# Down-sampled and banded attention followed by a gated expert layer on one core: nine equal token chunks instead of ten, with every queue written in a new order

## The chip, the cores and the metric

The kernel runs on 1 core of one Trainium2 chip. The metric is the device time of one execution in microseconds (us). TensorE is called PE, VectorE DVE, ScalarE ACT, GpSimd POOL, and SyncE, which issues all transfers here, SP. PE's clock has two levels, 1.2 and 2.4 GHz; the profile gives the level granted in a stretch as a share of the higher one.

## The reference

Attention runs over 8 batches of 8 heads, 576 positions and 64 values a head, and its result x (8 x 576 = 4608 tokens of 512 values) goes through a layer that mixes each token with the one before it:

```python
out_up    = repeat(softmax(mean4(q) @ mean4(k).T / 8) @ mean4(v), 4)   # per head
out_local = softmax(where(|i - j| < 4, q @ k.T / 8, -1e9)) @ v
x  = out_up + out_local                               # heads side by side: 512 values a token
xk = mu_k * x + (1 - mu_k) * x_prev                   # x_prev: the token before, in its batch
xr = mu_r * x + (1 - mu_r) * x_prev
k  = max(xk @ w_k, 0)                                 # 512 -> 1024
v  = (k * k) @ w_v                                    # 1024 -> 512
out = sigmoid(xr @ w_r) * v
```

## The kernel before, in words

**Attention.** The work is cut into 32 units n, two heads of one batch each; four units make a batch. For a unit, SP loads q, k and v (`load_raw`, `load_v4`, `load_windows`); the first six units turn q and k on PE (`flip`, L558) and copy the result out of the accumulation memory on ACT or DVE (`turn_part`, L423 and L427), later ones turn them on DVE. `run_pe(n)` issues in one piece on PE the scores of unit n (`score_pe`, L649 or L654), the down-sampled scores (L712) and the products of the unit before with its values (L805). DVE, ACT and POOL make the softmax, and `av_up`, `av_two` and `av_out` (L423, L877, L884) write the unit's part of x into one of two tiles `xt`, one a batch. After a batch's last unit, `av_pe` issues the value products alone.

**The layer.** The 4608 tokens are cut into chunks of 512 tokens (`CHUNKS`), two of them of 256 tokens only, at 2048 and at 4352. A chunk has one or two pieces of 256 tokens. For each piece DVE and ACT make xk and xr (`mix_prev`, `mix_part`), split into a high and a low part (`mix_high` L427 or ACT, `mix_low` L971), since every product is formed as high x high, high x low and low x high. For each of eight blocks f of w_k, `k_pe` (L983) issues twelve products whose moving operand is the whole chunk: 512 columns, or 256 in the two short chunks. ACT takes the maximum with 0, squares and rounds (L997, L1001, L1005), and DVE or POOL forms the low part (`k_low`, L1011). `v_pe` (L1040) issues, for a block f and a piece, six products of 512 columns, three for each of the piece's two tiles t of 128 tokens; they add up over f in one bank a tile. `r_pe` (L1020) issues twelve products of 512 columns a tile, `gate` (L1025) the sigmoid, `store_mul` (L1050) the last product on DVE, and `store_out` (L1054) the store. For the last tile of the program `columns` cuts the last block's products, the multiplication and the store in two halves of 256 columns.

**The weights.** Each of 20 weight tiles is loaded (L445), put together from two words on ACT and DVE (L450, L463, L467) and split into a high and a low part; for four of them PE forms the difference (`weight_diff`, L478 and L479). Before the program's first products, `warm` (L364) issues nine products of 512 columns on a cleared tile (`clear_warm`, L358).

**The order.** Every step is a task of a planner (`Plan.add`). The order in which tasks are issued, on all five engines, is a written-out list of task numbers (`ORDER`); `ELSE` moves named tasks to another engine. `Plan.arrange` walks that list, gives out the six accumulation banks, and the program then ties each engine's instructions into that order, so that every engine works strictly through its own queue. What waits for what follows from the data.

Of the kernel before, what the change touches and what calls it, by code (L numbers as in the profile page):

```python
# [51 lines left out]
0,4A5G1s5N0-3:1t5U5B5O0.5H490*1d5I151K4F4B1e5J4>1X5P3,5C165E4C1Y17184K1f4D4G5F5Q5Y0/4E1L505X1Z4r0:1a5Z4L5u5K5R5a
1M4t5L1N1b5v414s19591g1A4H1B4u5S1i3-3)4I5c1h4M1Q4J4N5n5V4v5d5o3<5e5f4O5h5p4P635g5i5z5y1O5j5q5k5W4w3&4Q3>1j1k4U64
5r1l5b1R1S6K4y1T5#4V4R654S5l3*5!1U5w4x3;5m1V5s4T5t5%6L661C3+1P4W1D4X6H3.424Y5+4z5&1m5(5,5x5)684!676N4Z1n5;6I3=69
5*5<6M815=4e5-5>5.6P607>615$4a6O6A4b4#4f6B4c826Q6C4d5/4$5:4g8U623/6R4h6D406E4%6S6T4i6U6V4j836k6J6X6q8V6d6o856m84
4l6Y6e8R6l6f6F6Z6n6G4&436r6p4(444k6s4)6u6t7=4m6w4p864+6&6g6W6+6)6(6-6*6a6h8S4*4n6i6,6!6.4q6b6j6/876c4o6:6x8E766#
8F6y8w6v8K7B774,8L8u788W888G6z8H8X8A8Y7Q8D8M807C8N8x798O7D8Z7L6$898P8B8Q4.4-967E8T8I8C8a7A8t8m7F7G8J8b8g8n8c8h8d
8e8y7s8z7H8o977M7t6%7N7I7u6;7J724/8i6=8#7K938j7v8f7k8p7O8!7R7SA&8k7P8v7x7l8q8l7w8r8s8$7T7U8;947y8%8<8+8&7zA#8(8,
70987V958*8-8)8.9ABC997a8=A(7W719B8>7X7#4;7b908/7Y8:917!7Z926<7c6>9C7d9OA$7$739D9P9E9FA)A%7%9QBF9G9I9V7mA*7e9X9J
BG9W9b9Z9c7f749K9a4:9YBh757nA+7&9d9f9HA,7g7o7h9g9h9e7i7j9p7(9R9r9t9l9v7)9L9w9u9S7q9m7p9s7+9q9M9x7*9i9N9j9T7r9UA-  # L60
9yA>BD9,BHB09k7-A:9n7,A=B59;9-BeBJB6B17.B7B2BiA6B89<A.BI9=9.B97;9/9oBKB,9>A1BA9:BBA/BfA;A<BLA2B37:BX7/B4AX9zBMBN
# [26 lines left out]
1!2J2p2x2>333V3Z3h565.6a8H8j8.9LBUBwC6E#FBF(HmH;IqKXKzL9Nk  # L88
""",
    DVE="""  # L90
0G0i0o0!0:1D1P1h1#1*1;2I2c2m2o2r32353D3M3Y3(3*3>494J4T4d555Z5!5&5:5<606s6y6/6;70727P8O8b8q8s8v8#8<959A9S9U9b9f9l
9z9#9%9(9*A+A,B6BEBJBYBbBlBoB(B+B;CACFCICMCOCQCSCWCiCkCsC:DsD!D&E7EpE(E+E:F0F1FFFKFNFkFmFvFxF,F/F;G3G5G7GFGHGJGL
GNGPGRGVHVHbHdHqHyH)I0IEIOISIXIfIgIuI$I)I+I/J2J4JAJIJfKGKLKMKOKeKjKoKrK%K+LGLLLRLiLpLrL#L(L<M5MQN7N9NINMNPNoNrNt
N+N=O4O6O8OAOGOKOMOOOQOSOUOWOYOaOvPWPaPcPePiPkPm
""",
    POOL="""
7A7F7K7U7eA5AKC+DAD<EMERGpGzG&JQJaJpMVOgOlOqO-O<PxP/P>Q9
# [9 lines left out]
class Plan:  # L107
# [64 lines left out]
    def lead(self, t, x):  # L172
# [148 lines left out]
def attention_moe(ctx: ExitStack, tc, q, k, v, mu_k, mu_r, w_k, w_v, w_r, band, ident, out):  # L321
# [706 lines left out]
    def v_pe(c, h, f):  # L1028
# [4 lines left out]
        if not (ended and c == NCH - 1):  # L1033
            todo.sort(key=lambda x: x[2] == 2)
# [140 lines left out]
    def both(keys):  # L1175
        return [x + y for y in keys for x in "hl"]
# [214 lines left out]
```

## Time and profile before

| | |
|---|---|
| time, median of 3 runs | 646.27 us (644.24 to 647.96) |
| profiled execution, its own time | 640.03 us |
| its span, first to last instruction | 638.2 us |
| instructions | 18038 |
| mean granted PE clock | 0.993 |
| bytes over HBM | 56.85 MB read, 13.86 MB written |

The span is what the page and the views of the trace describe; the profiled execution's own time is 1.8 us longer. Busy time of PE counts products whose ends are modelled; a matmul that is followed at once by another shows a longer time than the distance between their starts, so paces below are taken from starts.

### The profile page before, as it was taken

The page shows a single profiled execution, that of the slowest core. Times are in us where ns is not written, and L with a number is a line of the kernel's source. Part 1 is how long each engine was busy: PE and PEld are TensorE (multiplying, and loading weights), DVE is VectorE, ACT ScalarE, POOL GpSimd, SP SyncE. Part 2 cuts the span into 40 slices and gives each one's busy share as a digit, 9 for nine tenths or more (in the row PEclk, how much of TensorE's full clock was granted, in tenths as well). Part 3 has the DMA queues.
Part 4 walks back from the last instruction along what each step waited for, and adds up shares of the span by engine and source line. Part 5 has one row for each costly group of instructions (what it writes and reads, how often), then busy time and mean ns, then how long its engine had stood idle before and what let it go on. Part 6 is the DMA issues. An engine that isn't in the chain of part 4 may idle for free.

```text
span 638.2 us, 18038 instructions
## 1 busy us (share of the span) xinstructions
PE 621.7 (97%) x7034; PEld 514.7 (81%) x7034; DVE 483.5 (76%) x1039; ACT 400.1 (63%) x957; POOL 206.6 (32%) x285
## 2 busy tenths in 40 slices
PE   6799999999999999999999999999999999999997
PEld 5667788888888888888888888888888888888885
DVE  3969989888899979866799888978889757613133
ACT  3668867787677675766647576559667664334332
POOL 5757767536220451100430323012413320010110
PEclk9989999999999999999999999999999999999999
DMA  8888977556664656274354556635554330000001
GB/s 278 210 213 222 214 177 154 106 110 128 136 142 85 151 105 124 48 160 85 61 137 98 122 108 134 139 69 111 108 116 111 76 80 19 36 14 1 16 34 66
DMA packets 247127, 71.91 MB, mean 113 GB/s; under 512 B 219642, under 2 KB 238466, under 8 KB 247042
## 3 DMA queue, kind: packets, MB, share of 16 engines
q1 hardware_dynamic: 247042, 70.76, 49.4%
q8 instruction: 55, 0.90, 0.6%
q14 instruction: 30, 0.25, 0.1%
HBM read 56.85 MB, written 13.86 MB: 111 GB/s over the span
## 4 chain that ended last, share of the span: by engine, by line
PE 95%; issue 2%; DVE 1%; DMA 1%; ACT 0%; POOL 0%; SPq 0%; DVEq 0%; POOLq 0%
PE acc L1040 31%; PE ps_g L983 31%; PE ps_r L1020 16%; PE ps_v L805 5%; PE ps_a L712 3%; PE ps_a L649 3%; PE ps_f L558 1%; PE ps_a L654 1%; DMA wk<-in_moe_w_k_dram 1%; PE ps_m L926 1%; PE ps_w L478 1%; PE ps_t L762 1%; PE ps_t L767 0%; DVE ps_w L463 0%; ACT ad L729 0%
## 5 line engine op out<-in xcount | busy, mean ns | idle before, releaser
L983 PE MATMUL ps_g<-xks,wk 128*128 128x512 f32 (+1 forms) x960 | 206.9, 369 | 0.4 <-issue 0.4
L983 PEld LDWEIGHTS ps_g<-xks,wk 128*128 128x128 f32 x960 | 168.2, 188 | 32.6 <-issue 1.3
L1040 PE MATMUL acc<-wv,kh 128*128 128x512 f32 x578 | 157.3, 393 | 0.1
L1040 PEld LDWEIGHTS acc<-wv,kh 128*128 128x128 f32 x578 | 106.0, 188 | 21.9 <-PE ps_g L983 0.5
L1020 PE MATMUL ps_r<-wr,xr 128*128 128x512 f32 x432 | 103.7, 391 | 0.0
L1011 POOL TENSOR_TENSOR kl<-kk,kh 128x512 fp32r<-128x512 f32 (+1 forms) x35 | 42.3, 1209 | 180.3 <-ACT kh L1005 178.8
L1020 PEld LDWEIGHTS ps_r<-wr,xr 128*128 128x128 f32 x432 | 80.6, 188 | 17.0
L997 ACT ACTIVATE kk<-ps_g 128x512 f32<-128x512 f32 (+1 forms) x80 | 43.7, 549 | 79.9 <-PE ps_g L983 77.9
L1040 PE MATMUL acc<-wv,kl 128*128 128x512 f32 x289 | 89.2, 389 | 0.0
L918 DVE SCALAR_TENSOR_TENSOR mix<-xt,mus,mix 128x256 f32<-128x256 f32 (+3 forms) x184 | 68.9, 413 | 13.0 <-ACT mix L423 12.5
L1040 PEld LDWEIGHTS acc<-wv,kl 128*128 128x128 f32 x289 | 54.3, 188 | 11.6
L1011 DVE TENSOR_TENSOR kl<-kk,kh 128x512 fp32r<-128x512 f32 (+1 forms) x45 | 31.9, 708 | 40.4 <-ACT kh L1005 30.7
L1005 ACT ACTIVATE kh<-kk 128x512 fp32r<-128x512 f32 (+1 forms) x80 | 46.6, 585 | 18.7 <-PE acc L1040 17.4
L1001 ACT ACTIVATE kk<-kk 128x512 f32<-128x512 f32 (+1 forms) x80 | 45.8, 583 | 1.1
L423 ACT ACTIVATE mix<-xt,mus 128x256 f32<-128x256 f32 (+2 forms) x108 | 42.0, 439 | 5.0 <-DVE xr L971 2.4
L613 POOL TENSOR_TENSOR tk<-kz 64x288 f32<-64x288 f32 (+1 forms) x32 | 25.5, 796 | 54.0 <-DVE sd L736 20.1
L729 ACT ACTIVATE ad<-ps_a,mxd 128x144 f32<-128x144 f32 x96 | 35.3, 377 | 3.0 <-PE ps_v L805 1.2
L593 DVE STREAM_TRANSPOSE kz<-kraw 64x576 f32<-64x576 f32 x48 | 36.6, 762 | 0.7
L671 DVE TENSOR_TENSOR sm<-ps_a,mask 128x384 f32<-128x384 f32 x32 | 17.7, 552 | 24.9 <-PE ps_a L712 21.6
L1025 ACT ACTIVATE sig<-ps_r 128x512 f32<-128x512 f32 x36 | 21.2, 592 | 23.8 <-PE ps_r L1020 23.6
L805 PE MATMUL ps_v<-bd,vw 64*64 64x48 f32 x1536 | 35.9, 216 | 0.0
L805 PEld LDWEIGHTS ps_v<-bd,vw 64*64 64x64 f32 x1536 | 35.6, 134 | 0.0
(126 smaller groups left out, 952.0 us busy)
## 6 DMA issues: line engine op xcount, KB each, us to landing
vw<-in_v_dram SPq DMA_DIRECT2D x126, 96.0 KB, 2.9
out_dram<-sig SPq DMA_DIRECT2D x35, 256.0 KB, 2.4
v<-in_v_dram SPq DMA_DIRECT2D x32, 256.0 KB, 3.1
qraw<-in_q_dram SPq DMA_DIRECT2D x104, 72.0 KB, 2.5
kraw<-in_k_dram SPq DMA_DIRECT2D x104, 72.0 KB, 2.4
wk<-in_moe_w_k_dram SPq DMA_DIRECT2D x8, 512.0 KB, 5.8
wv<-in_moe_w_v_dram SPq DMA_DIRECT2D x8, 512.0 KB, 6.0
keys<-blocks SPq DMA_DIRECT2D x96, 40.0 KB, 1.8
```

The lines of the kernel that those rows point to most:

```text
L423: nc.scalar.activation(out, x, AF.Copy, **scale)
L593: nc.vector.transpose(kz[h, e, 3:579], raw[h])
L729: nc.scalar.activation(ad[:, x, :], ps[:, t, :], AF.Exp, scale=1.0 if n < LONG else 1.0 / 128, bias=mx[:, t:t + 1], accum_out=sd[:, x:x + 1])
L805: nc.tensor.matmul(pv[r][64 * e:64 * e + 64, cols], lhs, rhs, start=(i == 1), stop=(i == NG + 1 + (r != e)))
L918: nc.vector.scalar_tensor_tensor(out=to[:, p, o:o + L], in0=xts[b][:, p, s + 1:s + 1 + L], scalar=mu[:, p:p + 1], in1=to[:, p, o:o + L], o ...
L983: nc.tensor.matmul(kq[c, f], w_k_part(p, f, w), x[:, :, y, p, :], start=(m == 0), stop=(m == len(mm) - 1))
L997: nc.scalar.activation(kk, kq[c, f].rearrange("p h t -> p (h t)"), AF.Relu)
L1001: nc.scalar.activation(kq[c, f], kq[c, f], AF.Square)
L1005: nc.scalar.activation(kh, kk, AF.Copy)
L1011: engine().tensor_tensor(out=kl, in0=kk, in1=kh.bitcast(F32), op=ALU.subtract)
L1020: nc.tensor.matmul(ps, x[:, y, p, o:o + P], ws[f"r{p}"][:, w, :], start=(m == 0), stop=(m == len(mm) - 1))
L1040: nc.tensor.matmul(accs[c, t][:, j], x[:, o:o + P], ws[f"v{f}"][:, w, j], start=(f == 0 and m == 0), stop=(ended and m == 2), skip_group_c ...
```

## The change

The chunk table becomes nine chunks of 512 tokens, so all products of `k_pe` have 512 columns, and every chunk has two pieces. The last unit of value products (last chunk, last piece, last block) leaves `v_pe` and becomes three tasks `v_last`: one for the tile t = 2, and one for each half of t = 3. `store_mul` of a half then depends on that half alone. All of `ORDER` and `ELSE` is written anew.

```diff
-CHUNKS = [(0, 2), (512, 2), (1024, 2), (1536, 2), (2048, 1), (2304, 2), (2816, 2), (3328, 2), (3840, 2), (4352, 1)]
+CHUNKS = [(512 * c, 2) for c in range(9)]
...
 ORDER = """
-021u1x0400031v0J2A0C0A1z0k1$0K011#1!0L2B1(1%2E1&0D0M2g1)0e0N2F1+2G0E2h090F0l0X0B2K2H1<2I2J2/1,2k0m2L1-2l1=2:2m0Q
+00041u1v0e2A0k0A1z271x5D1!1$2B1#011(051%2E1&2g0f0X0g0l1)2F1+2h2G0C0B2K2H1<2k1,2J1=2/0m090w0Y0h2I2:0n1-2L2n0Z0a0D
...
     POOL="""
-7A7F7K7U7eA5AKC+DAD<EMERGpGzG&JQJaJpMVOgOlOqO-O<PxP/P>Q9
+7A7K7U7Z7j9:A0A5AFC%D0D5DADFFjF%F:IUIoItIyLKLPLoNuN&N,O1O=
...
         todo = [(t, j, m) for t in ts for j in (columns(c, t) if ended else columns(0, 0)) for m in range(3)]
-        if not (ended and c == NCH - 1):
-            todo.sort(key=lambda x: x[2] == 2)
+        todo.sort(key=lambda x: x[2] == 2)
...
+    def v_last(c, h, f, t, i):
+        kh, kl = kq[c, f]
+        j = columns(c, t)[i]
+        for m, (x, w) in enumerate([(kh, 0), (kh, 1), (kl, 0)]):
+            o = P * (t % 2) + (CT * SLOT[c, h] if CHUNKS[c][1] == 2 else 0)
+            nc.tensor.matmul(accs[c, t][:, j], x[:, o:o + P], ws[f"v{f}"][:, w, j],
+                             start=False, stop=(m == 2), skip_group_check=(j.start > 0))
+
     def columns(c, t):
-        n = 2 if (c, t) == (NCH - 1, 1) else 1
+        n = 2 if (c, t) == (NCH - 1, 3) else 1
...
+                if (c, h, f) == (NCH - 1, n - 1, NF - 1):
+                    for t in ts:
+                        m = len(columns(c, t))
+                        for i in range(m):
+                            add("PE", 0.847 if m == 1 else 0.52, v_last, c, h, f, t, i,
+                                r=[f"kh{c}.{f}", f"kl{c}.{f}"] + both([f"v{f}"]) + ([f"acc{c}.{t}"] if m > 1 else []),
+                                w=[f"acc{c}.{t}" if m == 1 else (f"acc{c}.{t}", i)])
+                    continue
...
-                add("DVE", 0.69 if m == 1 else 0.42, store_mul, c, t, i, r=[f"acc{c}.{t}"] + ([f"sig{c}.{t}"] if m > 1 else []),
+                add("DVE", 0.69 if m == 1 else 0.42, store_mul, c, t, i,
+                    r=[f"acc{c}.{t}" if m == 1 else (f"acc{c}.{t}", i)] + ([f"sig{c}.{t}"] if m > 1 else []),
```

Three places of the new order follow; names are those of the program's tiles, with the tile's own number behind an underscore.

The start of PE's queue before (ps_f: a turned q or k of a unit, ps_a: its scores, ps_x: the products of `warm`):

```order
L364 MATMUL ps_x<-xks 128x512 x9
L558 MATMUL ps_f<-small,qraw 64x64 x18
L558 MATMUL ps_f<-idn,kraw 64x64 x18
L558 MATMUL ps_f<-small,qraw 64x64 x18
L654 MATMUL ps_a<-kz_79,qT_86 32x32 x48
L712 MATMUL ps_a<-kd,qd_75 64x144 x6
```

and a later stretch of the same queue after the change, from the scores of the fifth unit to the value products of the third:

```order
L654 MATMUL ps_a<-kz_79,qT_86 32x32 x48
L712 MATMUL ps_a<-kd,qd_75 64x144 x6
L364 MATMUL ps_x<-xks 128x512 x9
L558 MATMUL ps_f<-idn,kraw 64x64 x18
L558 MATMUL ps_f<-small,qraw 64x64 x18
L805 MATMUL ps_v<-adT,vd 64x144 x4
```

The nine products of `warm`, first on PE before, now stand behind the scores of the fifth unit; PE's queue begins with the turns of q and k. On ACT, the copies of the first turned q and k now stand ahead of the first weight (L423 ahead of L450; before, one L450 came first).

PE's queue after the change where the last unit of attention hands over to the eighth chunk (ps_v: the last unit's value products; acc: values of the seventh chunk; ps_r: its gates; ps_g: the first products of the eighth chunk; the equal rows of the second piece and of the other parts of ps_r and ps_g are left out):

```order
L805 MATMUL ps_v<-adT,vd 64x144 x4
L805 MATMUL ps_v<-bd,vw 64x48 x9
L805 MATMUL ps_v<-adT,vd 64x144 x2
L805 MATMUL ps_v<-bd,vw 64x48 x15
L1039 MATMUL acc<-wv_2232,kh 128x512 x4
L1039 MATMUL acc<-wv_2232,kl 128x512 x2
L1020 MATMUL ps_r<-wr_1777,xr 128x512 x3
L983 MATMUL ps_g<-xks,wk_658 128x512 x3
```

Between the last value products and the first product of the next chunk stand 36 products of 512 columns (12 acc, 24 ps_r); before, at the same handover (to the ninth chunk there), 72 (36 acc, 24 ps_r, 12 ps_g).

The end of PE's queue before:

```order
L1040 MATMUL acc<-wv_1851,kh 128x512 x2
L1040 MATMUL acc<-wv_1851,kl 128x512
L1040 MATMUL acc<-wv_1851,kh 128x256 x2
L1040 MATMUL acc<-wv_1851,kl 128x256
L1020 MATMUL ps_r<-wr_1536,xr 128x512 x3
L1020 MATMUL ps_r<-wr_1595,xr 128x512 x3
L1020 MATMUL ps_r<-wr_1992,xr 128x512 x3
L1020 MATMUL ps_r<-wr_1421,xr 128x512 x3
```

and after:

```order
L1048 MATMUL acc<-wv_2232,kh 128x512 x2
L1048 MATMUL acc<-wv_2232,kl 128x512
L1020 MATMUL ps_r<-wr_1777,xr 128x512 x3
L1020 MATMUL ps_r<-wr_1845,xr 128x512 x3
L1020 MATMUL ps_r<-wr_1969,xr 128x512 x3
L1020 MATMUL ps_r<-wr_1673,xr 128x512 x3
L1048 MATMUL acc<-wv_2232,kh 128x256 x2
L1048 MATMUL acc<-wv_2232,kl 128x256
```

The last gate products move ahead of the two halves of the last tile's value products (the row pair of the second half is equal and left out).

## Rows read from the trace of the kernel before

**Rows 1.** The page, busy time, its share of the span and instructions of each engine.

```profile
PE 621.7 (97%) x7034; PEld 514.7 (81%) x7034; DVE 483.5 (76%) x1039; ACT 400.1 (63%) x957; POOL 206.6 (32%) x285
```

**Rows 2.** Stretches: us, busy of PE, PEld, DVE, ACT, POOL, PE clock, DMA share, GB/s.

```profile
16.00:32.00 16.00, 12.41 (x356) 9.95 (x356) 14.81 (x33) 10.89 (x31) 11.98 (x19) 0.91 0.87 210
...
80.00:96.00 16.00, 16.00 (x234) 13.43 (x232) 13.60 (x27) 10.83 (x28) 10.67 (x15) 1.00 0.78 176
```

**Rows 3.** Waits of PE: engine, tile, line, releaser: us in total, times, longest.

```profile
PE ps_a L712 <- issue: 4.3, 2, 2.2
PE ps_f L558 <- issue: 2.1, 2, 1.1
PE ps_f L558 <- ACT qT L423: 1.8, 1, 1.8
PE ps_a L654 <- issue: 1.5, 1, 1.5
```

**Rows 4.** Transfer queues on the page: packets, MB, share of 16 engines.

```profile
q8 instruction: 55, 0.90, 0.6%
```

**Rows 5.** Timeline of PE in the second short chunk: start, us, what.

```profile
604.49 1.09 PE L1040 MATMUL acc<-wv,kh 128*128 128x512 f32 x4
...
605.88 1.60 PE L983 MATMUL ps_g<-xks,wk 128*128 128x256 f32 x12
607.31 1.09 PE L1040 MATMUL acc<-wv,kh 128*128 128x512 f32 x4
```

**Rows 6.** The chain that ended last, two pieces of it: start, us, what.

```profile
105.45 5.44 PE ps_g L983 x24
...
259.20 5.44 PE acc L1040 x24
```

**Rows 7.** Timeline of the end.

```profile
630.89 2.91 PE L1020 MATMUL ps_r<-wr,xr 128*128 128x512 f32 x12
633.84 0.60 ACT L1025 ACTIVATE sig<-ps_r 128x512 f32<-128x512 f32 x1 [3.54 <-PE ps_r L1020]
634.47 0.76 DVE L1050 TENSOR_TENSOR sig<-acc,sig 128x256 f32<-128x256 f32 x2 [2.74 <-ACT sig L1025]
```

**Rows 8.** Timeline of PE and ACT at the start; in brackets the idle time before.

```profile
1.05 4.21 PE L364 MATMUL ps_x<-xks 128*128 128x512 f32 x9 [1.05 <-DVE xks L358]
5.19 1.26 PE L558 MATMUL ps_f<-small,qraw 64*64 64x64 f32 x36
...
7.96 0.62 ACT L450 ACTIVATE ps_w<-wk 128x512 f32<-128x512 f32 x1 [3.93 <-DMA wk<-in_moe_w_k_dram]
...
14.46 0.46 PE L712 MATMUL ps_a<-kd,qd 64*64 64x144 f32 x4 [2.13 <-issue]
14.70 1.61 PE L558 MATMUL ps_f<-idn,kraw 64*64 64x64 f32 x36
15.99 2.23 PE L558 MATMUL ps_f<-small,qraw 64*64 64x64 f32 x36
```

**Rows 9.** One stretch of 4 us, columns as in rows 2.

```profile
16.00:20.00 4.00, 3.73 (x149) 3.51 (x149) 4.00 (x9) 2.55 (x9) 2.74 (x5) 0.64 0.50 147
```

**Rows 10.** Timeline from the last unit's value products to the ninth chunk.

```profile
533.39 1.19 PE L1040 MATMUL acc<-wv,kh 128*128 128x512 f32 x4
...
534.15 0.82 DVE L884 TENSOR_TENSOR xt<-ps_v,up 128x288 f32<-128x288 f32 x2
...
534.89 0.47 DVE L425 TENSOR_SCALAR mix<-xt,mus 128x192 f32<-128x192 f32 x2
...
538.84 1.66 DVE L918 SCALAR_TENSOR_TENSOR mix<-xt,mus,mix 128x192 f32<-128x192 f32 x6
...
547.03 0.69 DVE L427 CAST xks<-mix 128x1024 fp32r<-128x1024 f32 x1
547.75 1.23 DVE L971 TENSOR_TENSOR xks<-mix,xks 128x1024 fp32r<-128x1024 f32 x1
...
549.84 2.88 PE L983 MATMUL ps_g<-xks,wk 128*128 128x512 f32 x12
```

More of the change, by code (lines that the diff above doesn't have):

```diff
@@ L52 @@
[L52 to L61, printed above, removed]
@@ new lines @@
+2!0q0G2X12352u0H0L2v2Y2#2Z3R0M1E1*373W0N0S0!0I2i0#3V0O3E0r082$4<240s0P4=0t2S2a252M26280$2T293X2w2%3F3Y2&2b2x2j13
+0T3Z383r3G140U153a180u2c0V2d3s3H3b2;392e2y0v1F3I3d2f2(2<3A1G2)3B031H2z3t5T0W3k2s1I543J3e5156363S3f2*533l524>3C3K
+2+57553u2,3D2-583T5X0%3g2.1J3h0&3L0(0+3c3x3M3m3N193O5U3v3P163%3i3n1A3!3o3j5u5Z3p3:3q3w5A591B0)3<0;3y5M173#1C5v3z
+3*0*5B3$4A0,5G5N5Y5H1o1D5C450-5E5a0<5I1W0.0=5J5y4F465F503+5O0>473,485z1p495V5P5K4B410/4K5Q1X1q1K4G1r0:5L5R3>1Y5!
+4C1c5S5c4D5#4E635h4L5b1Z1s4P3=1L5d5e5i1i1t5f1M641N664M4r5g4H401O104s5j1d5n115w1e4t5o4I1f5k5W4J4u1a4v676K4N4Q3(4U
@@ new lines @@
+4O4R5$651j1Q5p1k1l694x3)4V6H5q1g5r5l685s4w6L5m3&5t4W5%4S1m5x4T5;1h4z5&815+6J5(5,5)4y6M5<6N825*4Z5-3-1R3.4X5=6O4Y
+4#4a1n8U5.5>6A1b601S4e8R3;6P611T626I6B6Q3/4!4f6C425/7=4g4$5:4b6D4c1P6R6E4d1U1V6d4h4%6S6X6e6T6U4i6f846Y4j806V864l
+834k6k6g6o6F6m6p6G6n4&436h6q444(6r6u4n6l8V4m6Z6i6s6a4+6w6t6j6W4p6&6(6)856+7>6v6-6*4)6,4q6.6y8S6x6/876b4o6:8w8K76
+8T8W6c4,8L8X7B8M778N6!8E6#8F8x6z7G8O8Z8P784-7C8D8879898G8A7D8B7L7A8Q8H8u8Y6$4*8a8I7H4.7E6%8J7F7s8C7M6;8m7I7k8b7N
+8y8n8t8c8d8o8!8e8g967t8p8h8q7Q7J8i8f6=8r7K8z977l7v8s7R8#8j8v7u4/8k8$7O8l7S7P728;7w8%8<8&8(998=7xA#987V9B7T8*8>8)
@@ new lines @@
+6>7U938+7a908,9AA&917W8-8.707y7bA(926<9C8/95949O7z9D9P7X9EA)8:9Q7!9F7c9G9I9V7#9R7Y9Z9S7Z9b7m9TA$9JA*73A,9W4;7f4:
+71BF9c74757$7g9H9XA+7h7%9Y9UBG9f9a7d7q9KA%9h7i7eBh9d7j9i7&9eBD7n7(7r9l9p9v9r7)9q9LBe9j9t7o9M9u9N9s9w7+9x7*9m7p9g
+A-9yBC9kB59nA:9,A=A.B6A/A;BHBfB79o9;9-A>9.B87/9zBiBI9/B9B0BJAXBA7.BBBK7-9<B17,AVA<7:B2AY9=BEB3BLB4AW9:9(BXA1BMBY
+BN9#BRBOBSBQBP9$AeBjBZB)9>BaAdA2A0BkB,A6Bl9)BmBbB-AgA7Bc9%Bd9&BnBTBgDpBUA8A39!A49*AfA5BVBoBWAiBpA9BqBzAAABB.B!B+
+B#B$AhACBsBtB/ADAGAE7<BuB*AFB;BvB%AkAHDqBrB&AIB(AjB:9+DmB<C3BwAlB=AJB>C0AmC1BxCGDoDsByALCKCQC4DrAQC9AMCMDnAKCADt
@@ new lines @@
+N5MNNFLfMOLeMuMYMvL)LgNHM#LkMwMkLwMnMoL(LlMpLhMxMqM$NJM+L+M%M,M&M(L*M*M-LiM.LmLtN3M/LnM)LjLoM:M;L,LuNAL-NKNLM<NB
+L/M=M>N0N1L.NMNNNSO2NOL:NQL>NRNTNPO4NUNVNWL<NgNYNaOYNcNdNZNlOaNhNXNbNiNeNjNfNqNmOiOcNkNnObNoOoL=NvL;NrNpM0M2OpOd
+M1OkOZOBNwOeO5OfOANsOmODNtNuN!OCN#NxN$OFNyNzOEOHN%O3N&OGOJN-N(OIN)N*N<N+N.N,OLN=N/OgO8N:OhOnOsOKOuO9OvN>N;OyONOl
+OwOtOzOxO6OjO!O0O#O1OMOqOPOrOOO/OROQOTOXOUO>O:OVO;P4P0P1O<P2O=O7P3PgP5OSP6P9OWPhPiP7PAP8PBPjO$O)O%O&PkPCPDPJPEPl
+PFPKPLPmPGPHPnPIPoPMPNPpO(O*PaPrPOPqPPPQPYPRPSPtPZPbO+PsO,O-PTO.PcPUPVPWPXPuPdPvPzPeP!PyP(P%P&PwPfPxP#P$P)P*
@@ L194, in lead @@
             return 0.68 * p + (0.0 if m in ("weight_high", "weight_top") else 0.227 if n == "r_pe" else 0.45)
+        if n == "v_last":
+            return (0.24 if a[3] % 2 else 0.45) if m == "k_low" else 0.0
         if n == "v_pe":
```

54 lines of the change are left out of this document (21 added, 33 removed).

## The prediction

> **What bounds the kernel now.** Four views, in this order. First the busy times [rows 1]: PE is busy for 621.7 of 638.2 us, DVE, the next, for 483.5. So what counts is the length of PE's own queue, and the 16.5 us in which PE is idle. Second, the stretches [rows 2]: from 80 us on every stretch up to 620 us shows PE busy throughout (the row for 80 to 96 us stands for them; one of them lacks 0.06 us) at full clock, so nothing PE waits for is late there. Idle time lies in the first 80 us and in the last 4.4. Third, PE's waits [rows 3]: of the idle time at the start, 7.9 us in these rows is put down to "issue", no engine and no transfer; only 1.8 us waited for ACT. The instruction queue [rows 4] says what "issue" is here: 55 packets of 16 KB carry the 14,068 products and weight loads of PE [rows 1], 256 to a packet. In PE's timeline the waits lie some 254 instructions apart, or a multiple of that, and only where the queue holds short products: 36 turns take 1.26 us [rows 8], so a packet's worth is executed in 3 to 4 us, and PE then waits for the next. Long products, 0.227 us each, never wait. Fourth, the end [rows 7]: after PE's last product follow a sigmoid, a multiplication in halves and a store.
>
> **What the change removes: half-width products.** In the second short chunk [rows 5] the distance from 604.49 to 607.31 us, 2.82, holds six value products and twelve first products of 256 columns. Twenty-four products of 512 columns take 5.44 in either line [rows 6], so six take 1.36, twelve 2.72. The twelve half-width products thus take 2.82 - 1.36 = 1.46, not 1.36. There are 16 such groups, and 8 full groups take their place: 16 x 1.46 - 8 x 2.72 = 23.36 - 21.76 = **1.6 us less** of PE's queue, all of it on the path, since PE never waits there. By the Trainium skill ("TensorE: Matmul & The Clock Gate", section "Wait — 56ns, not 53.3ns?") a product costs a fixed 2.5 ns beside its columns; 96 fewer products would then be worth an estimated 0.24 us, and the sum below would be 638.6. The rows give 1.6, so I keep 1.6.
>
> ACT and DVE lose eight short steps of each kind and POOL takes over more of L1011; none of these engines is on the path [rows 1, 2], so I cost that at nothing. The cover is PE's queue; if it were gone, DVE would have 483.5 us of work, still far below the span.
>
> **The end.** Before, PE's last twelve products end with the start of the sigmoid at 633.84; the two halves are multiplied until 634.47 + 0.76 = 635.23, 1.39 later [rows 7]. After the change six products of 256 columns, 6 x 0.122 = 0.73 us, follow the last gate products and run beside that sigmoid (0.60) and the first multiplication. The second half starts after the first, so the stores leave at the same 1.39 us behind the gate products, while 0.73 us of PE's work has moved behind them: **0.7 less**. Bounds: 0.1 (the sigmoid's 0.60 still in series) to 0.73.
>
> **The start.** Three pieces, with bounds from near rows.
> - ACT's first weight step at 7.96 (0.62 us) no longer stands ahead of the copies of the turned q and k; the third turn waited 1.79 us for such a copy [rows 3, 8]. Also six banks are free for turns where `warm` held one before. **1.8 less**; bounds 0 and 1.8.
> - `warm` ran from 1.05 to 5.26, beside the first loads [rows 8]. Now the turns come first on a PE that has done nothing. At the lower level (the clock of 0.64 from 16 to 20 us is a mix of 1.2 and 2.4 GHz [rows 9]) two turns took 1.61 and 2.23 us, mean 1.92, not 1.26 [rows 8]. Two turns: 2 x 0.66 = **1.3 more**; bounds 0.7 and 1.9.
> - The nine products of `warm` now stand in the middle of the start: 9 x 0.227 = 2.0 us, or 4.2 at the pace of rows 8. By counting the new order, they fall into a packet's worth that holds 4.3 us of work with them and 2.3 without. The like packet before held 3.6 and then waited 1.0 for "issue", 4.6 in all. So the wait covers them: **0**; bounds 0 and 2.0, if that wait is not there.
>
> The "issue" waits themselves: priced by the same rows, PE's work up to the 3,492nd instruction is 74.6 us in both orders, and each has five or six packets of under 4.5 us. I take **no change**; bounds 4.3 either way, the two longest waits [rows 3]. SP's queue starts with one transfer (the identity) put ahead of q and two instead of three weights among the first loads; turns are waited for in both, and 0.5 us is the distance of two issues, inside the bounds above.
>
> **Sum.** 640.03 - 1.6 - 0.7 - 1.8 + 1.3 = 637.2 us for a profiled execution, 0.44% less. The median of the runs shown is 646.27, 1% above the profiled one; the same share off it gives **643.4**. About 0.5%, 3.2 us, is what a measurement of this kernel can tell from no change: 643.0 and 649.5 are the limits.
>
> **Rivals.**
> *Less waiting for instructions* (faster). If two of the long "issue" waits go, because weights (512 KB each) no longer crowd the first 8 us of transfers, 4.3 us more go: 643.4 - 4.3 = 639.1. For it: the short packets before were followed by waits of 0 to 2.2 us, so the wait depends on what else is being moved. Against: the new order has as many short packets, and moves the same bytes.
>
> *PE waits for the last batch's tokens* (slower). The eighth chunk now needs the last unit of attention, and PE's queue has only 36 products, 36 x 0.227 = 8.2 us, between that unit's value products and the chunk; before it was 72, 16.3. Before, PE came to the ninth chunk at 549.84, 16.4 us after those products ended at 533.39, and the tokens were ready at 547.75 + 1.23 = 548.98, 15.6 us after them [rows 10]. If that chain stays as long, PE waits 15.6 - 8.2 = 7.4: 643.4 + 7.5 = 650.9. Against: before, DVE mixed two pieces in that time and now one. By the new order the chain is 1.6 (to the end of L884), 0.5 (L425), eight L918 at 1.66 / 6 each, 2.2, one multiplication of 512 columns (two halves, 0.76 [rows 7]), 0.7 (L427) and 1.2 (L971): 7.0 us. It decides from 8.2 on; 1.2 us of anything unforeseen on DVE's queue shows as a wait.
>
> *A cold PE* (not faster). If the clock stays at 1.2 GHz past the two turns, up to the scores of the fourth unit, some 20 us of PE's work by the order run at 1.92 / 1.26 = 1.5 of their time: 10 us more, of which the "issue" waits there, up to 6, hide in it: 643.4 + 4 = 647.4. For it: PE now sits idle until q arrives. Against: the two turns of rows 8 at the lower level were themselves enough, the clock was up again before 20 us [rows 9]. The Trainium skill (same page, section "What's actually happening") has PE throttled by default until it has been busy; by that rule the first turns start at 1.2 GHz, as I have priced them, and no run here shows a start without `warm`.
>
> *The change does nothing* for the time: the half-width products' price lies in my reading of starts, and the start gives back the rest: 646.3.
>
> **Chances.** The sum as worked out 0.50 (own range 640.4 to 646.4, a shift of one or two "issue" waits); less waiting for instructions 0.20; the wait for the last batch 0.13; a cold PE 0.08; nothing 0.09. Faster by over 0.5% (under 643.0): 0.45 of the first case and nine tenths of the second, 0.225 + 0.18, 0.41. Slower (over 649.5): most of the third, part of the fourth and of the first's edge, 0.15. Within: 0.44. For eight times in ten I leave out the lower part of the second and the upper part of the third case: 637.5 to 650.5.
>
> **What would show it.** In the changed kernel L983 has one form, 864 products; the last PE row is a value product of 256 columns, with the sigmoid beside it. The first turn should start near 5 us and take about 1.9, the third should wait for no ACT copy. "Issue" waits should sum to 8 us, give or take 4. From 80 us to the end PE should be busy throughout; a wait of L983 for L971 around 515 to 530 us is the second rival. I am wrong if PE's idle time between 80 us and the end exceeds 2 us, or if PE's busy time does not fall by about 1.5 us.

## The result, and the profile after

| | before | after |
|---|---|---|
| median of 21 runs each | 643.34 us | 646.86 us |
| ratio, 95% interval | | 1.0073 (1.0047 to 1.0098) |
| profiled execution, its own time | 640.03 us | 648.47 us |
| PE busy, in the profile | 621.7 us | 625.0 us |
| instructions | 18038 | 17810 |

The change is **slower**, by 0.73%, or 4.7 us (3.0 to 6.3). The ratio is that of the fast executions alone (three of the 21 before, each over 1.5% above the fastest of that kernel, are left out), so it is larger than the 3.5 us between the two medians. The two profiled executions stand 8.4 us apart, since the one before lies below its median and the one after above it.

The page of the changed kernel, busy times [rows 1]:

```profile
PE 625.0 (97%) x6938; PEld 512.2 (79%) x6938; DVE 479.8 (74%) x994; ACT 389.3 (60%) x907; POOL 253.5 (39%) x340
```

96 products are gone from PE, and it is busy 3.3 us longer. PE's waits, the four largest [rows 3]:

```profile
PE ps_a L654 <- issue: 4.2, 2, 3.0
PE ps_f L558 <- DMA qraw<-in_q_dram: 4.2, 1, 4.2
PE ps_g L983 <- ACT kk L997: 3.1, 2, 2.4
PE ps_f L558 <- DMA kraw<-in_k_dram: 2.1, 1, 2.1
```

The third is new, and its largest part lies behind 80 us. The timelines of ACT and PE there (ACT's two rows first):

```profile
81.26 0.63 ACT L450 ACTIVATE ps_w<-wr 128x512 f32<-128x512 f32 x1 [2.10 <-DMA wr<-in_moe_w_r_dram]
81.82 0.58 ACT L997 ACTIVATE kk<-ps_g 128x512 f32<-128x512 f32 x1
...
79.55 0.52 PE L767 MATMUL ps_t<-idn,an 128*128 128x16 f32 x4
82.45 4.60 PE L983 MATMUL ps_g<-xks,wk 128*128 128x512 f32 x12 [2.39 <-ACT kk L997]
86.99 1.02 PE L654 MATMUL ps_a<-kz,qT 64*32 64x32 f32 x96
```

Read it backwards. PE waited 2.39 us for a bank; the bank was freed by ACT's maximum L997; that stood in ACT's queue behind a weight step L450; and that waited 2.10 us for its weight, one that no product reads before 126 us (L1020 first starts at 126.91). The stretches behind it show the second price, columns as in [rows 2]:

```profile
80.00:84.00 4.00, 1.61 (x5) 1.27 (x5) 3.88 (x8) 2.74 (x6) 2.38 (x3) 0.82 0.74 179
84.00:88.00 4.00, 4.00 (x110) 3.04 (x109) 2.38 (x5) 2.99 (x8) 3.77 (x6) 0.75 0.84 278
```

In and after the stretch in which PE was busy 1.61 of 4 us the granted clock (0.82 and 0.75) is a mix of 1.2 and 2.4 GHz; the twelve products took 4.60 us, where twelve take 2.88 [rows 10].

To place the loss, I use PE's starts of the scores of the sixth, ninth and fourteenth unit as marks. Up to the ninth and up to the fourteenth, both orders have issued the same products; up to the sixth, the changed order has issued twelve fewer (2.7 us). Before, then after:

```profile
66.94 1.02 PE L654 MATMUL ps_a<-kz,qT 64*32 64x32 f32 x96
115.51 0.88 PE L649 MATMUL ps_a<-kz,qT 128*32 128x64 f32 x48
199.59 0.88 PE L649 MATMUL ps_a<-kz,qT 128*32 128x64 f32 x48
```

```profile
68.10 1.02 PE L654 MATMUL ps_a<-kz,qT 64*32 64x32 f32 x96
122.80 0.88 PE L649 MATMUL ps_a<-kz,qT 128*32 128x64 f32 x48
207.75 0.88 PE L649 MATMUL ps_a<-kz,qT 128*32 128x64 f32 x48
```

Between sixth and ninth ("the middle" below) the kernel before takes 48.57 us. With twelve more products that makes 51.3; the changed one takes 54.70. From the ninth to the fourteenth it is 84.08 against 84.95, from there to PE's last start 433.8 against 434.8.

### The profile page after: what moved, and what is told of

Its sections match the earlier page's. It is cut to its first block, busy times and chain, and to the rows that moved or that the text cites. A ratio compares the mean times of both kernels' runs of the same rounds, so it can differ in the third digit from the quotient of the medians.

```text
span 646.7 us, 17810 instructions
## 1 busy us (share of the span) xinstructions
PE 625.0 (97%) x6938; PEld 512.2 (79%) x6938; DVE 479.8 (74%) x994; ACT 389.3 (60%) x907; POOL 253.5 (39%) x340
## 4 chain that ended last, share of the span: by engine, by line
PE 80%; DMA 5%; DVE 5%; ACT 4%; SPq 3%; issue 2%; POOL 1%; DVEq 0%; POOLq 0%; ACTq 0%
PE acc L1039 28%; PE ps_g L983 26%; PE ps_r L1020 13%; PE ps_v L805 4%; PE ps_a L712 3%; PE ps_a L649 3%; DMA kraw<-in_k_dram 2%; SPq L515 1%; PE ps_f L558 1%; DMA qraw<-in_q_dram 1%; DMA wr<-in_moe_w_r_dram 1%; PE ps_a L654 1%; SPq L541 1%; ACT ad L729 1%; DVE kz L593 1%
## 5 line engine op out<-in xcount | busy, mean ns | idle before, releaser
L983 PE MATMUL ps_g<-xks,wk 128*128 128x512 f32 x864 | 207.0, 393 | 3.1 <-ACT kk L997 3.1
L983 PEld LDWEIGHTS ps_g<-xks,wk 128*128 128x128 f32 x864 | 162.4, 189 | 38.4 <-ACT kk L997 3.6
L1020 PE MATMUL ps_r<-wr,xr 128*128 128x512 f32 x432 | 102.9, 390 | 0.1
L1011 POOL TENSOR_TENSOR kl<-kk,kh 128x512 fp32r<-128x512 f32 x40 | 53.1, 1327 | 126.2 <-ACT kh L1005 126.0
L997 ACT ACTIVATE kk<-ps_g 128x512 f32<-128x512 f32 x72 | 42.6, 594 | 96.9 <-PE ps_g L983 91.6
L1020 PEld LDWEIGHTS ps_r<-wr,xr 128*128 128x128 f32 x432 | 80.9, 188 | 17.9 <-ACT kk L997 0.6
L1039 PEld LDWEIGHTS acc<-wv,kl 128*128 128x128 f32 x286 | 53.5, 188 | 12.0 <-POOL kl L1011 0.7
L423 ACT ACTIVATE mix<-xt,mus 128x256 f32<-128x256 f32 (+3 forms) x122 | 46.4, 431 | 8.9 <-DVE xr L971 4.1
L1005 ACT ACTIVATE kh<-kk 128x512 fp32r<-128x512 f32 x72 | 44.9, 625 | 8.9 <-PE acc L1039 8.1
L1011 DVE TENSOR_TENSOR kl<-kk,kh 128x512 fp32r<-128x512 f32 x32 | 23.0, 719 | 36.4 <-ACT kh L1005 36.4
L1001 ACT ACTIVATE kk<-kk 128x512 f32<-128x512 f32 x72 | 44.3, 623 | 0.6
L746 POOL TENSOR_TENSOR an<-ad,sd 64x144 f32<-64x144 f32 (+2 forms) x56 | 31.4, 571 | 25.0 <-DVE sd L736 16.4
L971 DVE TENSOR_TENSOR xks<-mix,xks 128x1024 fp32r<-128x1024 f32 x16 | 20.2, 1263 | 27.4 <-ACT xks L423 27.3
L677 POOL TENSOR_TENSOR sm<-sm,mx 128x384 f32<-128x384 f32 x26 | 24.2, 932 | 40.1 <-DVE mx L672 35.3
```

The source lines that it names most:

```text
L423: nc.scalar.activation(out, x, AF.Copy, **scale)
L983: nc.tensor.matmul(kq[c, f], w_k_part(p, f, w), x[:, :, y, p, :], start=(m == 0), stop=(m == len(mm) - 1))
L997: nc.scalar.activation(kk, kq[c, f].rearrange("p h t -> p (h t)"), AF.Relu)
L1001: nc.scalar.activation(kq[c, f], kq[c, f], AF.Square)
L1005: nc.scalar.activation(kh, kk, AF.Copy)
L1011: engine().tensor_tensor(out=kl, in0=kk, in1=kh.bitcast(F32), op=ALU.subtract)
```

## The experiments

Ratios are to the kernel before, run on the same chip beside each, with 95% intervals. "Order of A up to unit n" means: the list `ORDER` begins with A's tasks up to the scores of that unit (with A's choice of engine for them), and goes on with the other kernel's tasks that are not yet in it.

### Where the loss lies

**e1**, the changed kernel with the start of the one before:

```diff
-ORDER = after
+ORDER = before up to unit 9, then after
```

> The changed kernel with the queues of the kernel before up to the scores of the ninth unit (some 115 us), and its own order from there on; PE has done the same products by then in both orders. Theory 1 (the loss is made in the start): the rest of the changed order is 1.6 us (half-width products) and 0.7 us (end) shorter, so 643.3 - 2.3 = 641.0 us, 0.996 of the kernel before. Theory 2 (the rest of the new order is slower, or the half-width products cost nothing): the time stays at that of the changed kernel, 1.007. In between: the saving of 2.3 us is not there but the start is the loss: 1.000.

Measured: 1.0104 (1.0047 to 1.0160), six runs. Against theory 1; but PE waited 1.5 us behind the joint for `xt`, a wait that neither kernel has there, and the section from the ninth to the fourteenth unit took 86.4 us.

**e2**, the converse:

```diff
-ORDER = before
+ORDER = after up to unit 9, then before
```

> The kernel before with the queues of the changed kernel up to the scores of the ninth unit, and its own order from there on. Theory 1 (the start): the scores of the ninth unit come 7.3 us later in the changed kernel's trace, so 643.3 + 7.3 = 650.6 us, 1.011 of the kernel before. Theory 2 (the rest): 1.000.

Measured: 1.0055 (1.0025 to 1.0086). The changed order of the first 120 us alone costs 3.5 us (1.6 to 5.5), which makes three quarters of the loss at the middle of that interval, and half of what theory 1 said.

**e3**, the changed kernel with the order before up to unit 5:

```diff
-ORDER = after
+ORDER = before up to unit 5, then after
```

> The changed kernel with the queues of the kernel before up to the scores of the fifth unit only (some 48 us), with the products of warm at the front again. In the traces these scores start 2.8 us later in the changed kernel, with 0.9 us more of PE's work done and the 2.0 us of warm still to do, which makes 3.9 us. Theory 1a (the first 50 us, the cold PE above all, lose 3.9 us, and the rest is lost at 80 us): 646.9 - 3.9 = 643.0, 0.9995 of the kernel before. Rival (PE only waits for loads and instructions that come when they come, so a faster first part waits longer behind it): no change, 1.007.

Measured: 1.0158 (1.0110 to 1.0206). The two orders don't fit there: PE waited 2.5 us for POOL's L623 and 2.0 us for ACT's L930, and the mean granted clock was 0.984. It says nothing on the theories.

**e5**, joined later, where the two lists differ by three tasks:

```diff
-ORDER = after
+ORDER = before up to unit 14, then after
```

> The changed kernel with the queues of the kernel before up to the scores of the fourteenth unit (some 200 us); from there its own order, with chunks of 512 and the split last unit. From these scores to PE's last instruction the traces show 433.8 us before and 434.8 in the changed kernel (the half-width products save 1.3 us, small waits take them back), and the end is 0.6 shorter. Theory (what is lost is lost before 200 us): 643.3 + 1.0 - 0.6 = 643.7, 1.0006 of the kernel before. Rival (the new order from 200 us on costs the 4.7 us): 1.007.

Measured: 1.0000 (0.9968 to 1.0031). Its marks:

```profile
67.46 1.02 PE L654 MATMUL ps_a<-kz,qT 64*32 64x32 f32 x96
116.45 0.88 PE L649 MATMUL ps_a<-kz,qT 128*32 128x64 f32 x48
200.44 0.88 PE L649 MATMUL ps_a<-kz,qT 128*32 128x64 f32 x48
```

This is the change itself, nine chunks and a split last unit, with the old order of the first 200 us. It costs nothing and brings nothing, to within 2 us: **the loss lies before 200 us**, and what was forecast to be gained behind that isn't seen either.

**e6 and e7**, the middle alone exchanged:

```diff
-ORDER = after
+ORDER = after up to unit 6, before up to unit 9, then after
```

> The changed kernel with the kernel before's order only between the scores of the sixth and of the ninth unit (some 67 to 120 us). The profiles of three kernels with the changed order there took 53.6, 54.7 and 56.0 us for it, and two with the order before 48.6 and 49.1 for work that is shorter by twelve products (2.7 us): so 2.3 to 4.7 us too long, 3.4 in the mean. Theory (the middle is the loss): 646.9 - 3.4 = 643.5, 1.002 of the kernel before. Rival (the waits come with the start, whatever the order there): 1.007.

```diff
-ORDER = before
+ORDER = before up to unit 6, after up to unit 9, then before
```

> The converse: the kernel before with the changed order between the scores of the sixth and of the ninth unit only. Theory (the middle is the loss): 643.3 + 3.4 = 646.7, 1.005 of the kernel before. Rival: 1.000.

Measured: 1.0266 (1.0235 to 1.0298) and 1.0148 (1.0116 to 1.0179). Both failed at the joint at the sixth unit: in e6 PE waited 10.6 us for L933, a step that the other order makes earlier, in e7 2.2 us for POOL's L746 and 1.3 us for DVE's L736, for which neither kernel waits there. Nothing follows for the theories.

### One late weight

**e4**, one load on SP:

```diff
 L445 DMA wv (v2)
-L515 DMA kraw (k of unit 8), x4
 L445 DMA wr (r3)
+L515 DMA kraw (k of unit 8), x4
```

> The changed kernel with one load moved: on SP, the first of the two r weights (L445) goes ahead of the strided load of k of the eighth unit instead of behind it. In the changed kernel's trace ACT waited 2.10 us for this weight at 81 us, the ReLU that stood behind it came late, PE waited 2.39 us for its bank, and the clock was at 1.2 GHz for the 3.4 us behind that wait, in which twelve products took 4.60 us instead of 2.88. Theory 1b: both go, 4.1 us less, 642.8 us, 0.999 of the kernel before; the granted clock from 80 to 88 us is 1. Rival (the next late load takes its place, or the time lost comes back as a wait for instructions): 1.007, with another wait of over 1.5 us before 100 us.

Measured: 1.0046 (1.0015 to 1.0077), 645.0 us. The wait for L997 in the middle fell to 0.41 us and the clock stayed up; the middle took 53.6 us. Some of the loss comes back, less than half of the 4.1 us expected (the interval also allows none): the next r weight came 2.16 us late on ACT, and PE now waited 1.13 us for `xt` from DVE.

**e9**, the steps instead of the load:

```diff
-ACT L450, DVE L463 and L467 for r3 and r0 ahead of the second and third L997
+the same steps 16 to 27 tasks later in ORDER (and L499 of v6 earlier, for its buffer)
```

> The changed kernel with ACT's and DVE's steps for the two r weights of 81 us (L450, L463, L467; no product reads these weights before 126 us) some 5 to 10 us later in their queues, so that the ReLUs that free PE's banks (L997) no longer stand behind two late transfers; SP's queue is as in the changed kernel. Theory (the loss between 67 and 120 us, 2.3 to 4.7 us in the profiles, is ACT waiting in order for late weights while PE's banks wait behind it): 646.9 - 3.4 = 643.5, 1.002 of the kernel before, and PE's waits for the ReLU fall from 3.1 us to under 1. Rival (PE waits for the next thing instead, DVE or tokens): 1.005 to 1.007.

Measured: 1.0060 (1.0026 to 1.0094). The rival holds. PE's waits between 60 and 122 us:

```profile
PE ps_v L805 <- DVE bd L425: 1.5, 1, 1.5
PE ps_t L762 <- DVE w L467: 0.8, 1, 0.8
PE acc L1039 <- DVE xt L884: 0.6, 2, 0.3
PE ps_t L762 <- ACT ps_w L450: 0.4, 1, 0.4
```

No wait for L997 is left, and three for DVE have come. The middle took 54.9 us, at a granted clock of 1.00. The longest of the three has a cause of its own. The two steps L425 that PE waited for, in the changed kernel and then in e9, with POOL's two rows beside them in e9:

```profile
104.55 0.81 DVE L425 TENSOR_SCALAR bd<-at,side 128x288 f32<-128x288 f32 x2
```

```profile
99.98 2.67 DVE L425 TENSOR_SCALAR bd<-at,side 128x288 f32<-128x288 f32 x2
99.70 1.49 POOL L1011 TENSOR_TENSOR kl<-kk,kh 128x512 fp32r<-128x512 f32 x1 [1.03 <-ACT kh L1005]
101.16 1.32 POOL L499 TENSOR_TENSOR wr<-w,wr 128x512 fp32r<-128x512 f32 x1
```

In e9 DVE does them wholly beside two steps of POOL, and they take 2.67 us in place of 0.81. So this wait seems to come from POOL's work at that moment and not from DVE's place in the order; no run moves POOL's steps to try it.

**e10**, the fault put into the kernel before:

```diff
-L445 DMA wr (r0)
 L515 DMA qraw, kraw (unit 7), x8
 L445 DMA wv (v6)
+L445 DMA wr (r0)
```

> The same fault put into the kernel before: on SP one r weight (L445) is issued behind the two strided loads of the seventh unit and one more weight instead of ahead of them, some 6 us later; nothing else is moved. ACT's L450 for it stands ahead of two ReLUs in the kernel before too. Theory: ACT waits 2 to 4 us for the transfer and PE for the bank, 643.3 + 2 to 4 = 645.3 to 647.3, 1.003 to 1.006 of the kernel before, with a wait of L983 for L997 near 80 us. Rival (PE's queue covers it): 1.000.

Measured: 1.0004 (0.9972 to 1.0035), and a middle of 49.4 us. But the fault did not show: in this profile PE came to the sixth unit only at 74.1 us, and ACT waited for no weight between 70 and 100 us. Over its twelve executions the order before has those 6 us of room for this load; what a weight that does come late costs there, the run doesn't tell.

### Warm

**e8**:

```diff
-        for _ in range(WARM):
+        for _ in range(1):
```

> The changed kernel with one product of warm in place of nine (they write a bank that nobody reads). Theory 2 (nothing hides them in the middle of the start: the nine took 2.35 us at L364): 8 / 9 x 2.35 = 2.1 us less, 644.8, 1.004 of the kernel before. Rival (the prediction's: a wait for instructions covers them): 1.007. Rival 2 (without them the clock falls once more): over 1.007.

Measured: 1.0057 (1.0031 to 1.0083), 1 us below the changed kernel, inside the intervals. The profile tells more. The turn that follows `warm` now waits:

```profile
48.79 1.26 PE L558 MATMUL ps_f<-idn,kraw 64*64 64x64 f32 x36 [1.77 <-DVE xks L933]
```

In the changed kernel the nine products took 2.35 us and this wait was not there. So they are mostly covered, but by a wait for DVE, not by one for instructions.

**e11**:

```diff
-warm first on PE
+warm behind the scores of unit 5 (the kernel before otherwise)
```

> The kernel before with warm (and its memset) moved to the place that it has in the changed kernel, behind the scores of the fifth unit; nothing else is moved. By the prediction's terms: the first turns run at 1.2 GHz, 1.3 us more, and the nine products in the middle cost 0 to 2.0, so 644.6 to 646.6, 1.002 to 1.005 of the kernel before. Rival (the start waits for loads and instructions whatever PE's clock; the starts of three profiles with the changed head were not later at the sixth unit): 1.000. Rival 2 (a cold PE that stays at 1.2 GHz past the second unit): over 1.006.

Measured: 1.0035 (1.0001 to 1.0069), 2.2 us, within the prediction's terms. The first two turns take 2.18 and 2.13 us against 1.26 [rows 8], near the 2.23 of a turn at the lower level there; the views list no lower clock for that stretch, so the level is read from the pace. The third still waits 1.14 us for its copy and takes 2.18 too.

### DVE

How much of the middle each engine works (stretch from mark to mark, columns as in [rows 2]), before, after and e9:

```profile
66.94:115.51 48.57, 48.16 (x703) 39.71 (x702) 44.80 (x87) 38.14 (x97) 34.32 (x44) 1.00 0.81 168
```

```profile
68.10:122.80 54.70, 52.31 (x716) 43.29 (x715) 46.57 (x92) 38.34 (x100) 36.87 (x45) 0.97 0.87 176
```

```profile
63.39:118.32 54.93, 52.02 (x716) 42.17 (x715) 50.12 (x92) 38.47 (x100) 37.79 (x45) 1.00 0.91 178
```

DVE is busy 92% of the middle in the kernel before, though 76% of the whole [rows 1]; in the changed order it is busy for 1.8 us more there, with five more instructions, and for 5.3 in e9. The last step, from 46.57 to 50.12 us, is not more work: it is the same 92 instructions, some of them longer, as the two L425 above.

**e13 and e14**, less of DVE's work:

```diff
-        nc.vector.tensor_scalar(out=wi, in0=wi, ...
+        n = 1 if i >= 8 else 512
+        nc.vector.tensor_scalar(out=wi[:, 0:n], in0=wi[:, 0:n], ...
```

> The changed kernel with DVE's shift of a weight (L463) done on one of 512 columns for twelve of the twenty weights, eight of which are treated between the scores of the sixth and of the ninth unit: some 5 us less of DVE's work there, nothing moved on any queue; the weights' low bits of the other 511 columns are left out, so those twelve weights are not the reference's. Theory D (DVE bounds that stretch): most of the 3.5 us comes back, 646.9 - 3 = 643.9, 1.002 of the kernel before. Rival (ACT and late transfers bound it): 1.007.

> The same cut in the kernel before (the same twelve weights, the same columns left out). Both theories: PE is idle there for only 0.4 to 0.8 us, and up to the sixth unit it waits for instructions and ACT, so 0 to 1 us less, 0.998 to 1.000. Over 2 us less would mean that DVE sets the start as well.

Measured: 1.0034 (1.0006 to 1.0063) and 0.9972 (0.9943 to 1.0000). Both kernels become faster, by some 2.5 and 1.8 us; e14's profile has no shorter middle (48.6 us) to show for it. With the same cut in both they are as far apart as without it: 3.6 us between the medians (645.30 and 641.74), 3.5 in the result. So DVE's work costs time in both orders, but this much of it doesn't account for what parts them. It was also less than expected: in the middle DVE is busy for 44.31 us in e13, 2.3 less than in the changed kernel and not 5, since other steps took longer there. And in the profile the changed kernel's middle stayed at 55.0 us, and its one large wait in the middle was again the one of the first fence of ACT and PE above (L998 is L997 here, a line lower):

```profile
PE ps_g L984 <- ACT kk L998: 2.8, 1, 2.8
```

**e15**, more of it, in the kernel before:

```diff
         nc.vector.tensor_scalar(out=wi, in0=wi, scalar1=3, ...
+        if i >= 8:
+            nc.vector.tensor_scalar(out=wi, in0=wi, scalar1=0, ...
```

> The kernel before with that shift done twice (the second one by 0 bits) for the same twelve weights: eight more DVE instructions of 0.69 us between the sixth and the ninth unit, 5.5 us on top of 44.8 of 48.6. Theory D: DVE has some 3.8 us of slack there, so 1.7 us at least and 5.5 at most, 1.003 to 1.009. Rival (PE's queue covers it): 1.000.

Measured: 1.0064 (1.0028 to 1.0100), 4.1 us. Theory D holds: the middle went from 48.6 to 54.4 us, with DVE busy 52.0 of them.

```profile
64.80:119.21 54.41, 50.19 (x703) 39.82 (x702) 52.00 (x97) 38.39 (x97) 33.23 (x44) 1.00 0.75 161
```

That DVE has next to no slack there in the order before is shown.

**e16**, six steps from DVE to ACT:

```diff
 ELSE DVE
-L427 of v1, v2, r0; L425 (blocks) of units 6, 7; L427 of one xr
```

> The changed kernel with six of DVE's steps between the sixth and the ninth unit done by ACT instead, in the same places of the order (three casts of a weight's high part, two L425 of a unit's blocks, one cast of a mix): 3.4 us less on DVE by the plan's durations, 4.9 more on ACT, which is busy 38.3 of 54.7 us there. Theory D: 2 to 3 us less, 1.003 to 1.004 of the kernel before. Rival (ACT bounds it): 1.007 to 1.012.

Measured: 1.0040 (1.0007 to 1.0073), as theory D had it, but with a middle of 55.0 us in the profile, in which PE waited 2.2 us for L997.

### Both, and the price of a half-width product

**e17 and e18**:

```diff
 after
+e9 (steps of r3 and r0 later)
+e13 (L463 on one column)
```

```diff
 after
+e4 (load of r3 earlier)
+e9
+e16 (six steps on ACT)
+e8 (one product of warm)
```

> The changed kernel with both: ACT's and DVE's steps for the two r weights later in their queues, and DVE's shift (L463) on one column of 512 for twelve weights (the low bits of the other columns are left out). Theory E (two queues in order, each late by the same amount, bound the stretch between the sixth and the ninth unit): it takes 51 to 52.5 us instead of 55, and the time is 646.9 - 3.4 - 1 = 642.5, 0.999 of the kernel before. Rival (a third cause): 53.5 to 55 us there, 1.003 to 1.006.

> The changed kernel with four moves that leave the computation as it is: the first r weight's load ahead of a strided one, the two r weights' steps later, six of DVE's steps done by ACT, one product of warm instead of nine. Theory E: the stretch takes 52 to 53 us, 646.9 - 2.5 - 1 = 643.4, 1.001 of the kernel before; below 0.997 it would beat both. Rival (moving work to ACT delays the ReLUs instead): 1.004 to 1.007.

Measured: 1.0037 (1.0008 to 1.0065) and 1.0028 (0.9998 to 1.0058). The middle took 53.5 and 53.8 us, shorter than with either cause alone taken away by the cut or by the steps (54.9 to 55.0), but no shorter than in e4 (53.6), which moves one load, and not the 51 to 53 of theory E. e17 is what the rival, a third cause, had said; e18 lies between the two. In e17 the waits that end last are still of both kinds, for DVE on PE and for one more weight on ACT (waits of PE and ACT between 60 and 122 us):

```profile
PE ps_t L762 <- DVE w L467: 1.5, 1, 1.5
```

```profile
ACT ps_w L450 <- DMA wv<-in_moe_w_v_dram: 3.4, 1, 3.4
```

That third weight, a wv, was not tried. No version of the change with the full computation beat the kernel before; e5 equals it.

**e12** (its halves start their sums in one bank, so k isn't summed as in the reference):

```diff
-                nc.tensor.matmul(kq[c, f], w_k_part(p, f, w), x[:, :, y, p, :], ...
+                for s in range(2):
+                    nc.tensor.matmul(kq[c, f][:, s], w_k_part(p, f, w), x[:, s, y, p, :], ...
```

> The changed kernel with each of its 864 first products of 512 columns issued as two of 256. By the spacing of the half-width products in the kernel before (0.1200 us in the mean over 192 of them, 0.2267 for 512 columns) 864 x (2 x 0.1200 - 0.2267) = 11.5 us more: 658.4, 1.023 of the kernel before. By the prediction's price of 1.6 us for 96 pairs, 14.4 us more: 661.3. By the 2.5 ns a product of the Trainium skill (TensorE: Matmul & The Clock Gate, section Wait — 56ns, not 53.3ns?) 2.2 us more: 649.1, 1.009.

Measured: 1.0268 (1.0194 to 1.0342), 659.5 us, two runs. Against the changed kernel 12.6 us more, 14.6 ns for each of 864 pairs. PE's timeline, e12 and then after:

```profile
305.93 5.92 PE L984 MATMUL ps_g<-xks,wk 128*128 128x256 f32 x48
311.68 1.09 PE L1040 MATMUL acc<-wv,kh 128*128 128x512 f32 x4
```

```profile
302.76 5.60 PE L983 MATMUL ps_g<-xks,wk 128*128 128x512 f32 x24
308.20 1.07 PE L1039 MATMUL acc<-wv,kh 128*128 128x512 f32 x4
```

From start to start 5.75 us for 48 halves, 5.44 for 24 whole ones: 13 ns a pair. So 96 pairs are worth 1.2 to 1.4 us, near the rows' price. By the 2.5 ns a product of the Trainium skill ("TensorE: Matmul & The Clock Gate", section "Wait — 56ns, not 53.3ns?") it would be an estimated 0.24 us; for these products the measurement differs, and decides.

## Why the prediction was wrong

0.44% less was forecast and 0.73% more was measured. The 646.86 us lie inside the stated range all the same, but only because the kernel before, 646.27 us in the three executions shown, has a median of 643.34 in 21.

**Half-width products**, 1.6 less: the mechanism is right, the size 1.2 to 1.4 (e12). But PE's busy time did not fall, and from the fourteenth unit to PE's last start it takes 434.0 us in e5, with the saving, and 433.8 before, without. Three stops of PE in e5, 0.60, 0.33 and 0.31 us beyond the usual distance of the starts, take back 1.2 of it, and all three end on POOL:

```profile
227.52 0.58 PE L712 MATMUL ps_a<-kd,qd 64*64 64x144 f32 x9 [0.53 <-POOL kd L614]
242.78 0.58 PE L712 MATMUL ps_a<-kd,qd 64*64 64x144 f32 x9 [0.26 <-POOL qd L605]
283.74 0.30 PEld L1039 LDWEIGHTS acc<-wv,kl 128*128 128x128 f32 x2 [0.57 <-POOL kl L1011]
```

From the fourteenth unit on POOL is busy for 95.0 us before and for 140.5 in e5 (columns as in [rows 2]):

```profile
199.59:638.00 438.41, 434.15 (x4108) 362.88 (x4107) 317.02 (x684) 254.11 (x587) 94.99 (x121) 1.00 0.40 87
```

```profile
200.44:638.00 437.56, 433.31 (x4012) 358.09 (x4011) 308.16 (x633) 245.22 (x545) 140.52 (x175) 1.00 0.40 87
```

The prediction named more L1011 for POOL (26 there before, 30 after); the larger part is L746 (12 and 36) and L677 (6 and 15). I had costed all of it at nothing. The changed kernel has stops at the places of the second and third as well, and two more, of 0.8 and 0.4 us, for ACT's L997 and L423. That POOL's new work makes these stops is read from the waits; no run takes it away.

**The end**, 0.7 less: right. From PE's last start to the end of the span it is 4.15 us after and 4.81 before. PE's last products run beside the sigmoid, as said:

```profile
639.23 2.88 PE L1020 MATMUL ps_r<-wr,xr 128*128 128x512 f32 x12
642.14 0.60 ACT L1025 ACTIVATE sig<-ps_r 128x512 f32<-128x512 f32 x1 [4.16 <-PE ps_r L1020]
642.54 0.28 PE L1048 MATMUL acc<-wv,kl 128*128 128x256 f32 x1
642.91 0.76 DVE L1057 TENSOR_TENSOR sig<-acc,sig 128x256 f32<-128x256 f32 x2 [2.14 <-ACT sig L1025]
```

**The start**, 0.5 less: near in two terms, and better than forecast in its sum. The first two turns took 2.18 and 1.86 us (1.5 more, 1.3 said), and the third waited 0.32 for ACT instead of 1.79. `warm` was mostly covered, but by a wait for DVE and not for instructions (e8), so that term came out by luck; alone, moving it costs 2.2 us (e11, 0.1 to 4.4). "Issue" waits, for which I took no change, fell: 2.3 to 5.1 us in ten profiles with the changed start (6.9 in e12, which has more products), 6.6 to 10.9 in eight with the one before. (That long products never wait so was misread: L983 waits 0.41 us for "issue" at 71.31 in the kernel before.) The 2.1 us for a late k was not foreseen. Over the five profiles of each order at the start, the sixth unit's scores came at 61.4 to 68.1 us with the changed one and at 66.9 to 74.1 before, for 2.7 us less work.

**The step that failed** is the one behind the start: that from 80 us on nothing PE waits for is late, and that ACT, DVE and POOL can be costed at nothing because "none of these engines is on the path". The rows behind it [rows 1, 2] are of the order before. The stretch from 80 to 96 us did show PE busy throughout, but in that order, and with DVE busy 13.60 of 16 us in it. In the new order the middle is 2.2 to 4.8 us too long in all nine profiles with nothing added to it (53.5 to 56.1 us against 51.3), whether PE arrives at 61 or at 68 us and whether the clock falls or not. The start's gain is lost there, and more. From the ninth unit on, where 2.3 us less was forecast, 1.0 to 1.2 more came; the stops of PE behind the fourteenth unit are some 1.9 of that. DVE's lack of slack is shown for the order before (e15); that late weights on ACT hold PE in the changed one beside it is what the waits of the changed kernel and of e13 show, and e9, where DVE waits come when those go. How much each gives to the loss is not shown, nor that they are all: with both reduced (e17, e18) 2.2 to 2.5 us stay of some 3.5, and POOL, beside which DVE's steps took longer in e9, was left as it was.

My own test in the prediction was 2 us of idle time behind 80 us; it was 3.8 (2.39, and 1.4 from the ninth unit to PE's end); and PE's busy time rose by 3.3 us where it should have fallen by 1.5. **The rivals**: less waiting for instructions came, some 5 us by the profiles above, but other waits at the start and in the middle took its place. No wait appeared where the last batch's tokens are handed over; PE is busy throughout from 480 to 620 us. A cold PE did not decide: over 21 runs of the changed kernel and the 23 of the one before beside e1 the mean granted clock is 0.992 and 0.991, so the clock doesn't part them, though it spreads both. In none of my cases was the middle itself the place.

The profiles add up to less than the measured loss: in the start 2 to 3 us gained, in the middle 3.5 lost, from the ninth unit to the end 1.0 to 1.2 lost. That makes some 2 us, against 4.7 (3.0 to 6.3), or 3.5 between the medians. The start differs by 7 us from one execution to the next of the same order, and a profile is one execution, so the rest may be that; it stays open.

## What to carry to other kernels

A row that shows an engine busy throughout speaks for the order in which the other queues stood, not for the engine: when a change writes all queues anew, ask in each stretch for the second-busiest engine's share there (92% here, 76% over the whole), and cost its moves, and those of every engine that PE takes something from, however idle it is on average (POOL: 39% busy, and the end of all three stops in e5). In queues that are worked strictly in order, look for a step that nobody needs yet and that stands, with its load, ahead of one that frees a bank; here it cost PE 2.39 us in one profile, though moving it gave back less (e4, e9) and a later load cost nothing where the queue had room (e10). And to find where a change of order loses, join the two orders where they have done the same work: a joint where they have not (e3, e6, e7) makes waits of its own.

## What the runs showed that I had not expected

- The same program's start varies by several us: the kernel before took 637.6 to 651.9 us over these runs, with the granted clock from 0.98 to 1.0. Of the changed order's variants, a profile with a mean clock of 1.000 (e9, span 643.4 us) was no faster than one with 0.993 (e16, 640.9).
- Taking away one wait or the work before it gave back half of its length or less, and by the intervals perhaps nothing (e4, e8, e9): the next wait stood right behind it.
- Steps of DVE took longer where POOL worked beside them: L425 on 128x288 takes 0.37 us in the median of 30 in e9, and 1.38 us at the most.
